# Decode attention: how the last of eight head groups is normalised, turned into rows and written

## The chip, the cores and the metric

The kernel runs on one core of a Trainium2 chip. The metric is the device time in microseconds (us) of one execution. The experiments ran on several chips: b2, a2, rows16 and early28 on chip 7, hyb, pet, w4q and join3 on chip 1, stride8 and a3 on chip 5, probe on chip 6; for the first result none is recorded. Each ratio is taken against the kernel before on the same chip.

A profile covers a "span", from the first to the last instruction. It is 1.8 us shorter than the device time (634.0 against 635.79 in the profiled run of the kernel before). In profiles PE is the matmul engine (TensorE) and PEld its weight load, DVE is VectorE, ACT ScalarE, POOL GpSimd and SP SyncE; a "q" marks an engine's sequencer, which waits and issues DMAs. L195 is line 195 of that run's kernel, so the same step has different line numbers in different runs.

## The reference

One query position, 32 query heads, 8 key/value heads, 65536 keys of 128 elements, bf16:

```python
B, Hq, Hkv, Sq, Sk, D = 1, 32, 8, 1, 65536, 128
...
k = jnp.repeat(k, rep, axis=1)          # rep = 4
v = jnp.repeat(v, rep, axis=1)
scores = jnp.einsum("bhqd,bhkd->bhqk", q, k) * D ** -0.5
p = _softmax(scores, axis=-1)
return jnp.einsum("bhqk,bhkd->bhqd", p, v)
```

The work is reading 268 MB of K and V once. Four query heads share one K/V head; below, "head" with its index `h` of 0 to 7 is such a group of R = 4 query heads. Each is done in C = 2 blocks of 32768 keys, so there are N = 16 blocks. The two blocks of a head are joined with the usual rescaling of a running softmax.

## The kernel before

Each block's products p·V are summed in PSUM (the memory that matmuls write to) as *columns*: 128 partitions (the elements d of the output) by 4 (the query heads). V is the stationary operand (128x128 weights), the probabilities are the 4 moving columns:

```python
def values(tiles):
    for t in tiles:
        ins = pe.matmul(
            acc[:, 0:R], lhsT=vbuf[:, t * D:(t + 1) * D], rhs=pts[:, t * R:(t + 1) * R],
            start=t == 0, stop=t == T - 1,
        )
        if t % TH == TH - 1:
            ins.then_inc(pv_s, 1)
```

The last V block's second half is loaded in five pieces of 64, 32, 16, 8 and 8 tiles (`VLAST`), so that few products are left when the last byte lands. In the kernel before, the last 16 tiles change form: they are summed as *rows* (4 partitions by 128), with the probabilities stationary and V moving, so that the result can be written without a transpose. The columns collected so far are added by a matmul with an f32 identity, the sum of the probabilities is made by a matmul with ones:

```python
pe.matmul(acc[:, 0:R], lhsT=zero, rhs=zero[:, 0:R], start=False, stop=True)
pe.matmul(fsum[0:R, 0:1], lhsT=rhead, rhs=ones, start=True, stop=True).then_inc(fo_s, 1)
for n, a, b in list(pieces(VLAST, TH))[-NROW:]:
    pe.wait_ge(vlast_in[n], 16)
    for t in range(a, b):
        ins = pe.matmul(
            row[0:R, 0:D], lhsT=pts[:, t * R:(t + 1) * R], rhs=vbuf[:, t * D:(t + 1) * D],
            start=t == T - TG, stop=t == T - 1,
        )
    if n == len(VLAST) - NROW:
        pe.wait_ge(co_s, N)
        pe.matmul(row[0:R, 0:D], lhsT=o2, rhs=ident, start=False, stop=False)
ins.then_inc(pv_s, 1)
```

The other 7 heads (28 query heads) are transposed by VectorE in 32x32 blocks and written some 20 us before the end, by four writes from ScalarE's queue. The last head is scaled by ScalarE and written as 4 rows of 256 B:

```python
ac.wait_ge(ox_s, 1)
for a in range(A):                                   # A = 4
    ac.dma_start(
        of[0:Hq - R, a * S4:(a + 1) * S4], oX[a * S4:a * S4 + Hq - R, :],
    ).then_inc(o_out, 16)
ac.wait_ge(rc_s, H)
ac.wait_ge(pv_s, 2 * N)
ac.activation(olast, row[0:R, 0:D], AF.Copy, scale=rrow[0:R, :]).then_inc(ol_s, 1)
ac.wait_ge(ol_s, 1)
ac.dma_start(of[Hq - R:Hq, :], olast).then_inc(o_out, 16)
ac.wait_ge(o_out, 16 * (A + 1))
```

## Time and profile before

| | |
|---|---|
| time | 636.11 us, median of 3 runs (636.04 to 636.58) |
| span of the profiled run | 634.0 us |
| bytes | 268 MB, 424 GB/s |
| busy: PE, DVE, ACT | 43%, 54%, 44% |

The kernel is bound by its loads. Two lines of the page say so: the busy share of the 16 DMA engines in 40 equal slices of the span (a digit is tenths, 9 is 90% or more), and the shares of the chain of work that ended last.

```profile
DMA  9999999999999999999999999999999999999995
...
DMA 48%; DVE 27%; PE 15%; another core or an unknown queue 9%; issue 1%; SPq 1%; POOL 0%; ACT 0%; ACTq 0%
```

Only the last slice is not full. What the change touches all lies there, or is hidden. So the part to read is the chain of waits at the end (start in us, length in us, what it was; "issue" is time in which the engine waited for nothing that the profile shows):

```profile
614.09 14.69 DMA vbuf<-in_v_dram
628.78 0.05 issue
628.83 0.59 PE acc L195 x16
629.42 0.09 issue
629.50 0.16 PE acc L243
629.67 0.12 PE fsum L244 x2
629.79 0.87 PE row L248 x8
630.66 0.43 PE row L254 x2
631.09 0.87 PE row L248 x8
...
632.04 0.36 ACT ktb L408
```

and the same stretch in the timeline (start, length, engine, line, operation, output and inputs, their shapes, count):

```profile
628.83 0.59 PE L195 MATMUL acc<-pts,vbuf 128*128 128x4 bf16 x16 [0.22 <-DMA vbuf<-in_v_dram]
...
629.65 1.01 PE L248 MATMUL row<-vbuf,pts 128*4 128x128 bf16 x8
...
630.46 0.63 PE L254 MATMUL row<-ktb,small 128*4 128x128 f32 x2
...
630.89 1.06 PE L248 MATMUL row<-vbuf,pts 128*4 128x128 bf16 x8
632.04 0.36 ACT L408 ACTIVATE ktb<-row,small 4x128 bf16<-4x128 f32 x1 [15.65 <-PE row L248]
632.43 0.26 ACTq L410 DMA_DIRECT2D out_dram<-ktb  x1
```

A row product is slow: 8 of them take 1.01 to 1.06 us, where 16 column products take 0.59 (one row product starts every 107 ns, one column product every 27 ns). The trace also records when each DMA engine reports its share of a transfer as complete (a "landing"). The last V piece landed at 630.06 us; 15 of its 16 engines had landed by 627.77. From the last landing to the end of the span it is 3.93 us. I call this the *tail*; it is the part of the kernel that the change is meant to shorten:

| part of the tail, before | us |
|---|---|
| last V landing (630.061) to last matmul (631.945) | 1.88 |
| last matmul to issue of the last write (632.43) | 0.49 |
| issue to the write's last landing (633.58) | 1.15 |
| landing to the end of the span (633.995) | 0.41 |

### The profile page before, as it was taken

What the parts mean: (1) busy time and instruction counts of PE and PEld (TensorE: products, weight loads), DVE (VectorE), ACT (ScalarE), POOL (GpSimd) and SP (SyncE); (2) the same over time, 40 slices, a digit from 0 to 9 for tenths busy, and PEclk for the clock granted to TensorE, in tenths of its full rate; (3) what the DMA queues carried; (4) which work ended last, traced back from release to release, by engine and by line L of the source; (5) the groups of instructions that cost most, each with busy time, mean ns of one, the idle gap of its engine ahead of it and who ended that gap; (6) DMA issues with size and microseconds to landing.
All of it is one profiled execution on the core that took longest, in us unless ns stands there. A gap on an engine that the chain in (4) does not pass through costs nothing.

```text
span 634.0 us, 18764 instructions
## 1 busy us (share of the span) xinstructions
PE 271.7 (43%) x8197; PEld 245.2 (39%) x8197; DVE 341.0 (54%) x411; ACT 276.2 (44%) x1179; POOL 10.3 (2%) x33
## 2 busy tenths in 40 slices
PE   1314536144361534626255261553614437146535
PEld 1214436144361433525245261452614436146425
DVE  4649166390853809447193571926619176295710
ACT  1456425164351734617255261542616426165720
POOL 0000000000000000000000000000000000000000
DMA  9999999999999999999999999999999999999995
GB/s 365 429 450 418 443 430 435 438 426 438 422 447 426 438 426 435 438 422 447 418 455 418 442 431 426 442 422 443 422 455 410 451 426 434 430 410 437 430 359 219
DMA packets 6867, 268.68 MB, mean 424 GB/s; under 512 B 1088, under 2 KB 1088, under 8 KB 1728
## 3 DMA queue, kind: packets, MB, share of 16 engines
q1 hardware_dynamic: 6480, 268.44, 98.4%
q8 instruction: 5, 0.08, 0.1%
q14 instruction: 14, 0.11, 0.0%
q10 hardware_dynamic: 368, 0.04, 0.0%
HBM read 268.47 MB, written 0.01 MB: 423 GB/s over the span
## 4 chain that ended last, share of the span: by engine, by line
DMA 48%; DVE 27%; PE 15%; another core or an unknown queue 9%; issue 1%; SPq 1%; POOL 0%; ACT 0%; ACTq 0%
DMA kbuf<-in_k_dram 30%; DVE ktb L284 25%; DMA vbuf<-in_v_dram 17%; PE acc L195 13%; PE qkb L184 2%; DVE small L291 1%; SPq L119 1%; PE row L248 0%; POOL small L165 0%; PE row L254 0%; DVE small L335 0%; ACT ktb L408 0%; DVE small L317 0%; DVE small L313 0%
## 5 line engine op out<-in xcount | busy, mean ns | idle before, releaser
L284 DVE STREAM_TRANSPOSE ktb<-kbuf 128x1024 int32<-128x1024 int32 x256 | 295.8, 1213 | 161.2 <-DMA kbuf<-in_k_dram 158.2
L375 ACT ACTIVATE scs<-qkb 32x64 f32<-32x64 f32 x1024 | 220.5, 215 | 281.3 <-PE qkb L184 270.1
L184 PE MATMUL qkb<-qblk,ktb 128*128 x4096 | 157.3, 176 | 343.0 <-DVE ktb L284 330.3
L184 PEld LDWEIGHTS qkb<-qblk,ktb 128*128 128x128 bf16 x4096 | 132.9, 105 | 367.2 <-issue 199.0
L195 PE MATMUL acc<-pts,vbuf 128*128 128x4 bf16 x4080 | 112.0, 166 | 17.2 <-DMA vbuf<-in_v_dram 16.7
L195 PEld LDWEIGHTS acc<-pts,vbuf 128*128 128x128 bf16 x4080 | 110.4, 104 | 18.9 <-DMA vbuf<-in_v_dram 15.1
L291 DVE TENSOR_REDUCE small<-scs 128x4 f32<-128x256 f32 x64 | 38.0, 593 | 61.4 <-ACT scs L375 61.4
L392 ACT ACTIVATE pts<-scs,small 128x256 bf16<-128x256 f32 x64 | 48.9, 852 | 34.8 <-PE acc L195 34.8
L160 POOL PARTITION_ALL_REDUCE small<-small x16 | 6.0, 372 | 574.8 <-DVE small L302 574.8
L392 ACT ACTIVATION_READ_ACCUMULATOR pts<-scs,small 128x1 f32 x64 | 13.6, 212 | 0.0
L325 DVE COPY small<-acc 128x4 f32<-128x4 f32 x8 | 1.3, 162 | 22.3 <-PE acc L195 22.3
L381 ACT ACTIVATE small<-small 128x4 f32<-128x4 f32 x16 | 3.3, 205 | 21.8 <-POOL small L160 21.8
L313 DVE TENSOR_TENSOR small<-small 128x4 f32<-128x4 f32 x8 | 1.3, 163 | 18.1 <-PE acc L195 18.1
L331 DVE TENSOR_TENSOR small<-acc,small 128x4 f32<-128x4 f32 x8 | 1.2, 155 | 13.0 <-PE fsum L244 13.0
L408 ACT ACTIVATE ktb<-row,small 4x128 bf16<-4x128 f32 x1 | 0.4, 358 | 15.7 <-PE row L248 15.7
L307 DVE TENSOR_TENSOR small<-small 128x4 f32<-128x4 f32 x8 | 1.3, 164 | 4.0 <-POOL small L160 4.0
L165 POOL PARTITION_ALL_REDUCE small<-small x7 | 3.0, 432 | 18.5 <-DVE small L317 18.5
L302 DVE TENSOR_REDUCE small<-small 128x4 f32<-128x16 f32 (+1 forms) x16 | 2.9, 184 | 0.6
L335 DVE RECIPROCAL small<-small 128x4 f32<-128x4 f32 x7 | 1.2, 178 | 3.4 <-POOL small L165 3.4
L315 DVE TENSOR_TENSOR small<-small 128x4 f32<-128x4 f32 x8 | 1.3, 156 | 2.7 <-ACT pts L392 2.7
L365 ACT ACT_TABLE_LOAD x1 | 1.3, 1283 | 2.7 <-issue 2.7
L248 PE MATMUL row<-vbuf,pts 128*4 128x128 bf16 x16 | 2.1, 308 | 0.0
(27 smaller groups left out, 11.4 us busy)
## 6 DMA issues: line engine op xcount, KB each, us to landing
vbuf<-in_v_dram SPq DMA_DIRECT2D x3, 4096.0 KB, 25.5
kbuf<-in_k_dram SPq DMA_DIRECT2D x5, 2048.0 KB, 40.6
kbuf<-in_k_dram SPq DMA_DIRECT2D x1, 4096.0 KB, 22.4
vbuf<-in_v_dram SPq DMA_DIRECT2D x1, 2048.0 KB, 11.8
kbuf<-in_k_dram SPq DMA_DIRECT2D x2, 512.0 KB, 4.8
kbuf<-in_k_dram SPq DMA_DIRECT2D x1, 1024.0 KB, 7.3
vbuf<-in_v_dram SPq DMA_DIRECT2D x1, 1024.0 KB, 13.9
vbuf<-in_v_dram SPq DMA_DIRECT2D x1, 512.0 KB, 14.7
```

The costliest lines, as they stand in the source:

```text
L119: sp.dma_start(buf[:, a * D:b * D], src(t, i)[:, a * D:b * D]).then_inc(s, 16)
L160: g.partition_all_reduce(mtot if b else mfirst, hmax[:, b * R:(b + 1) * R], P, bass.bass_isa.ReduceOp.max,).then_inc(hma_s, 1)
L165: g.partition_all_reduce(lsum, rhead, P, bass.bass_isa.ReduceOp.add).then_inc(ls_s, 1)
L184: ins = pe.matmul(qkb[g // GU][:, at:at + A * R], lhsT=kt[:, be // NE, be % NE, n * P:(n + 1) * P], rhs=qblk[:, bass.ds(qcols[be], A * R)] ...
L195: ins = pe.matmul(acc[:, 0:R], lhsT=vbuf[:, t * D:(t + 1) * D], rhs=pts[:, t * R:(t + 1) * R], start=t == 0, stop=t == T - 1,)
L248: ins = pe.matmul(row[0:R, 0:D], lhsT=pts[:, t * R:(t + 1) * R], rhs=vbuf[:, t * D:(t + 1) * D], start=t == T - TG, stop=t == T - 1,)
L284: dv.transpose(to.rearrange("p (b t j) -> p b t j", b=NB, t=TG), fr.rearrange("p (t b i) -> p b t i", b=NB, t=TG),).then_inc(tr_s, 1)
L291: dv.tensor_reduce(hp[j % C][:, u * R:(u + 1) * R], scs[:, u * W:(u + 1) * W].rearrange("p (n g) -> p g n", g=R), AX.X, ALU.max,).then_inc ...
L302: dv.tensor_reduce(hmax[:, b * R:(b + 1) * R], hp[b].rearrange("p (u g) -> p g u", g=R), AX.X, ALU.max,).then_inc(hm_s, 1)
L375: ins = ac.activation(to[a * S4:(a + 1) * S4, x, :, :], fr[x * S4:(x + 1) * S4, a, :, :], AF.Copy)
L381: ac.activation(negb[b], mtot if b else mfirst, AF.Copy, scale=-scale).then_inc(nb_s, 1)
L392: ac.activation(pv[:, g_, :], sv[:, g_, :], AF.Exp, bias=negb[b][:, g_:g_ + 1], scale=scale, accum_out=rsum[h % 2][b][:, g_:g_ + 1],).then ...
```

## The change

All heads end as columns. The last two pieces use the same column products as the others. The first block's rescaled part joins PSUM by a matmul with the identity as weights, before these two pieces. The sum of the probabilities uses the partition all-reduce of the other heads. Then one multiply, one transpose of all 32 heads and one write from SyncE's (SP's) queue. The four early writes, the row form, the sum by matmul and ScalarE's scaling are gone. The intent is a shorter tail: cheap products at the end, and one write where there were five. The core of the diff:

```diff
@@ sync
+        sp.wait_ge(ox_s, 1)
+        sp.dma_start(of.rearrange("h (a i) -> a h i", a=A), oX).then_inc(o_out, 16)
+        sp.wait_ge(o_out, 16)
@@ gpsimd (... the all-reduce in a helper `total`, called once more at the end)
+        total(H - 1)
@@ tensor
-        pe.wait_ge(tail_s, 3)
-        pe.wait_ge(rh_s, H)
-        pe.matmul(acc[:, 0:R], lhsT=zero, rhs=zero[:, 0:R], start=False, stop=True)
-        pe.matmul(fsum[0:R, 0:1], lhsT=rhead, rhs=ones, start=True, stop=True).then_inc(fo_s, 1)
-        for n, a, b in list(pieces(VLAST, TH))[-NROW:]:
+        pe.wait_ge(tail_s, 2)
+        pe.wait_ge(ow_s, H)
+        pe.matmul(acc[:, 0:R], lhsT=ident, rhs=o2, start=False, stop=False)
+        for n, a, b in list(pieces(VLAST, TH))[-NEND:]:
             pe.wait_ge(vlast_in[n], 16)
-            for t in range(a, b):
-                ins = pe.matmul(row[0:R, 0:D], ...)
-            if n == len(VLAST) - NROW:
-                ...
-        ins.then_inc(pv_s, 1)
+            values(range(a, b))
@@ vector
-        dv.wait_ge(fin_s, H - 1)
+        weigh(H - 1)
+        dv.wait_ge(ls_s, H)
+        dv.reciprocal(recip, lsum).then_inc(rc_s, 1)
+        dv.wait_ge(rc_s, H)
+        dv.wait_ge(pv_s, 2 * N)
+        dv.tensor_tensor(oT[:, Hq - R:Hq], acc[:, 0:R], recip, ALU.mult).then_inc(fin_s, 1)
+        dv.wait_ge(fin_s, H)
         dv.transpose(oX, oT).then_inc(ox_s, 1)
-        collect(N - 1)
-        dv.reciprocal(rrow[0:R, :], fsum[0:R, 0:1]).then_inc(rc_s, 1)
@@ scalar
-        (the four early writes, the scaling and the write of the last head, as shown above)
```

More of the change, by code (lines that the diff above doesn't have):

```diff
@@ L22 @@
 VLAST = (64, 32, 16, 8, 8)
-NROW = 2
+NEND = 2
 HALVED = 2
@@ L41, in bass_standalone__gqa_softmax__decode_kernel @@
     scale = float(D) ** -0.5
-    assert sum(VLAST) == TH and sum(VLAST[-NROW:]) == TG
+    assert sum(VLAST) == TH and sum(VLAST[-NEND:]) == TG
     kf, vf = k[0], v[0]
@@ L74, in bass_standalone__gqa_softmax__decode_kernel @@
     rsum = [[cols(R) for _ in range(C)] for _ in range(2)]
-    warm, ones, rrow = cols(10), cols(1), cols(1)
+    warm = cols(10)
     assert used[0] <= 160
@@ L80, in bass_standalone__gqa_softmax__decode_kernel @@
     ident = ktb[0][:, 0:2 * P].bitcast(DT.float32)
-    zero = ktb[1][:, 0:P]
-    olast = ktb[1][0:R, P:P + D]
     qkb = [S(nc.psum_tensor(f"qkb{i}", [P, 512], DT.float32)) for i in range(U)]
     acc = S(nc.psum_tensor("acc", [P, 512], DT.float32))
-    row = S(nc.psum_tensor("row", [P, 512], DT.float32))
-    fsum = S(nc.psum_tensor("fsum", [P, 512], DT.float32))
     def sem(name):
@@ L101, in bass_standalone__gqa_softmax__decode_kernel @@
         sem("ls_s"), sem("co_s"), sem("ow_s"), sem("rw_s"), sem("rh_s"), sem("rc_s"), sem("fin_s"))
-    fo_s, ol_s, ox_s, tail_s = sem("fo_s"), sem("ol_s"), sem("ox_s"), sem("tail_s")
+    ox_s, tail_s = sem("ox_s"), sem("tail_s")
     init_s, pool_s, qt_s, qb_s, warm_s = sem("init_s"), sem("pool_s"), sem("qt_s"), sem("qb_s"), sem("warm_s")
@@ L149, in _, with total @@
             load_v(j - 1)
+        sp.wait_ge(ox_s, 1)
+        sp.dma_start(of.rearrange("h (a i) -> a h i", a=A), oX).then_inc(o_out, 16)
+        sp.wait_ge(o_out, 16)
     @block.gpsimd
     def _(g):
+        def total(h):
+            g.wait_ge(rh_s, h + 1)
+            g.partition_all_reduce(lsum, rhead, P, bass.bass_isa.ReduceOp.add).then_inc(ls_s, 1)
         g.wait_ge(init_s, 2)
         g.partition_all_reduce(warm[:, 4:8], warm[:, 0:4], P, bass.bass_isa.ReduceOp.max).then_inc(pool_s, 1)
-        g.memset(ones, 1.0).then_inc(pool_s, 1)
         g.memset(oTX[:, :], 0.0).then_inc(pool_s, 1)
@@ L163, in _ @@
             if b == 0 and n >= C:
-                g.wait_ge(rh_s, n // C)
-                g.partition_all_reduce(lsum, rhead, P, bass.bass_isa.ReduceOp.add).then_inc(ls_s, 1)
+                total(n // C - 1)
         g.wait_ge(qk_s, N * G)
-        g.memset(zero, 0.0).then_inc(tail_s, 1)
         g.memset(ident, 0.0).then_inc(tail_s, 1)
-        g.wait_ge(tail_s, 2)
+        g.wait_ge(tail_s, 1)
         g.affine_select(
@@ L232, in _ @@
                 pe.wait_ge(vb_in, late_ * 16)
-                for n, a, b in list(pieces(VLAST, TH))[:-NROW]:
+                for n, a, b in list(pieces(VLAST, TH))[:-NEND]:
                     pe.wait_ge(vlast_in[n], last_ * 16)
@@ L238, in _ @@
             pe.reg_add(turn, turn, 1)
-        pe.wait_ge(tail_s, 3)
-        pe.wait_ge(rh_s, H)
-        pe.matmul(acc[:, 0:R], lhsT=zero, rhs=zero[:, 0:R], start=False, stop=True)
-        pe.matmul(fsum[0:R, 0:1], lhsT=rhead, rhs=ones, start=True, stop=True).then_inc(fo_s, 1)
-        for n, a, b in list(pieces(VLAST, TH))[-NROW:]:
-            pe.wait_ge(vlast_in[n], 16)
-            for t in range(a, b):
-                ins = pe.matmul(
-                    row[0:R, 0:D], lhsT=pts[:, t * R:(t + 1) * R], rhs=vbuf[:, t * D:(t + 1) * D],
-                    start=t == T - TG, stop=t == T - 1,
-                )
-            if n == len(VLAST) - NROW:
-                pe.wait_ge(co_s, N)
-                pe.matmul(row[0:R, 0:D], lhsT=o2, rhs=ident, start=False, stop=False)
-        ins.then_inc(pv_s, 1)
+        pe.wait_ge(tail_s, 2)
+        pe.wait_ge(ow_s, H)
+        pe.matmul(acc[:, 0:R], lhsT=ident, rhs=o2, start=False, stop=False)
+        for n, a, b in list(pieces(VLAST, TH))[-NEND:]:
+            pe.wait_ge(vlast_in[n], 16)
+            values(range(a, b))
     @block.vector
@@ L321, in collect @@
             h, b = divmod(i, C)
-            if i < N - 1:
-                dv.wait_ge(pv_s, (i + 1) * 2)
+            dv.wait_ge(pv_s, (i + 1) * 2)
             if b == 0:
@@ L327, in collect @@
             weigh(h)
-            if i == N - 1:
-                dv.wait_ge(fo_s, 1)
             dv.wait_ge(ow_s, h + 1)
             dv.tensor_tensor(o2, acc[:, 0:R], o2, ALU.add).then_inc(co_s, 1)
-            if i == N - 1:
-                return
             dv.wait_ge(ls_s, h + 1)
@@ L400, in _ @@
             exponent(j)
-        ac.wait_ge(ox_s, 1)
-        for a in range(A):
-            ac.dma_start(
-                of[0:Hq - R, a * S4:(a + 1) * S4], oX[a * S4:a * S4 + Hq - R, :],
-            ).then_inc(o_out, 16)
-        ac.wait_ge(rc_s, H)
-        ac.wait_ge(pv_s, 2 * N)
-        ac.activation(olast, row[0:R, 0:D], AF.Copy, scale=rrow[0:R, :]).then_inc(ol_s, 1)
-        ac.wait_ge(ol_s, 1)
-        ac.dma_start(of[Hq - R:Hq, :], olast).then_inc(o_out, 16)
-        ac.wait_ge(o_out, 16 * (A + 1))
     es.close()
```

## The prediction

> **What bounds it now.** The loads. The page gives DMA 9 tenths in 39 of 40 slices, 424 GB/s; the chain of waits is 48% DMA. PE is 43% busy, DVE 54%, ACT 44%. The change rewrites only the tail after the last loads, so I price that from the timeline and the DMA landings (span 634.0 us).
>
> The last V pieces land on 16 engines, one late: the 16-tile piece at 628.78, the first 8-tile piece at 629.43, the last at 630.06 (15 engines had that last piece by 627.77).
>
> **Tail before** (timeline): acc x16 ends 629.42; clearing matmul (L243), sum matmul (L244), then 8 row matmuls 629.65 to 630.66, the f32 join (L254) 630.46 to 631.09, 8 row matmuls 630.89 to 631.96.  ACT scales at 632.04 (0.36), the write is issued 632.43 (0.26), first packet 633.17, landed 633.58, end 634.00. From the last load to the last matmul: 1.90 us, since row matmuls of 128 columns come every 94 to 123 ns, while the acc form runs 64 in 1.84 us (28 ns each).
>
> **Tail after, estimated from those numbers.**
> - acc x16 ends 629.42. The identity join, two f32 passes with 128x128 weights: 0.3 to 0.5 us, estimated from L254's 128 ns weight loads and L244's 0.19 for two passes. It ends near 629.9, before the last piece lands: hidden.
> - First 8 tiles end about 630.2. Last piece 630.06, its 8 tiles: 8 x 28 ns plus 0.14 drain (as x16 took 0.59) end near 630.48.
> - DVE multiply by the reciprocal 0.16 (L331's size) plus semaphore, transpose 0.20 (L355): oX ready near 630.93.
> - SP issues one write of 128 rows of 64 B: 0.43 (SP's other issues of 128 rows; 4 rows took 0.26). Start to first packet 0.74 for 4 rows, 1.0 for the 128-row first load; I take 0.95. Each of 16 engines does 8 packets of 11 ns (the early 64 B writes), landing 0.35 later: about 632.45. The closing barrier 0.42: end 632.85.
>
> Row matmuls: 1.9 us shrinks to 0.4; ACT's 0.36 becomes DVE's 0.4 in two steps; the write costs about 0.3 more. Net about -1.1 us, all on the critical path. All-reduce of the last sums (0.43) and the reciprocal (0.18) move to about 617, off the path (last rhead is at 616.8).
>
> Removed too: four early writes (112 rows of 64 B, beside the last V loads). The late engine's 16 packets of 8192 B from 620.11 to 625.04 took 16 x 309 ns, so they seem to cost it nothing.
>
> The Trainium skill, "DMA: Bandwidth & Descriptors", "Why a DMA increments its semaphore by 16 and not by 1", says the engine count comes from the row count: 128 rows use 16, 4 rows use 4; the trace agrees, the last write has 4 landings. Its "Specifications" says writes under 512 B are read-modify-write; 64 B rows may land later than 256 B ones. No isolated one is in the trace: the largest doubt.
>
> **Prediction: 635.0 us** against 636.11, range 634.3 to 636.0. Faster by over 2%: 0.005; within 2%: 0.99; slower: 0.005.
>
> **Right or wrong shows in:** L195 matmuls ending about 0.4 us after the last landing; last packet-to-landing near 0.35; no ACT work after 617; span near 632.9.
>
> **What would make it wrong:** instruction fetches (8192 B, 309 ns) fall differently on the late engine, moving the last landing by 0.3 us steps; the join costs over 0.6 us; the 128-row write lands 0.5 us later.

## The result, and the profile after

The changed kernel took 636.0 us (median of 6 runs, 635.65 to 636.23) against 636.12 us (6 runs, 635.97 to 636.58). The ratio is 0.9997, 95% interval 0.9984 to 1.0009: no difference that these runs can show. (A ratio is the mean time of one kernel's runs over that of the other's of the same rounds, so not quite the ratio of the medians quoted.) Instead of the forecast gain of 1.1 us, 0.1 us was seen. The profiled span was even longer, 634.3 us against 634.0.

The end of the changed kernel's chain of waits:

```profile
614.28 15.34 DMA vbuf<-in_v_dram
629.62 0.05 issue
629.67 0.59 PE acc L196 x16
630.26 0.10 issue
630.36 0.56 PE acc L244 x2
630.92 0.44 PE acc L196 x16
...
631.45 0.17 DVE oTX L346
631.62 0.02 issue
631.65 0.21 DVE oTX L348
```

and its timeline:

```profile
630.36 0.56 PE L244 MATMUL acc<-small,ktb 128*128 128x4 f32 x2
...
630.77 0.57 PE L196 MATMUL acc<-pts,vbuf 128*128 128x4 bf16 x16
631.45 0.16 DVE L346 TENSOR_TENSOR oTX<-acc,small 128x4 bf16<-128x4 f32 x1 [13.72 <-PE acc L196]
631.65 0.21 DVE L348 STREAM_TRANSPOSE oTX<-oTX 128x32 bf16<-128x32 bf16 x1
631.88 0.68 SPq L147 DMA_DIRECT2D out_dram<-oTX  x1
```

Two things are to be seen. First, the DMA line at the top of the chain ends at 629.62 and not at 628.78: that is the landing of the 16-tile piece, and the last piece follows in the same way, at 630.90 and not at 630.06. The loads ended 0.84 us later, though nothing in the loads was changed. Second, the last matmul ends at 631.34 (before: 631.95) in spite of that, but the write is issued for 0.68 us, not for 0.26, and lands late:

| part of the tail | before | predicted | after |
|---|---|---|---|
| last V landing to last matmul | 1.88 | 0.42 | 0.44 |
| last matmul to issue of the write | 0.49 | 0.45 | 0.54 |
| issue to the write's last landing | 1.15 | 1.52 | 2.02 |
| landing to end | 0.41 | 0.40 | 0.39 |
| sum (the tail, us) | 3.93 | 2.79 | 3.40 |

(The sums are taken from the unrounded times. The predicted column subtracts the times that the prediction gives: 630.06, 630.48, 630.93 (transposed rows ready, taken as the issue), 632.45, 632.85.) So 1.45 us were won at the products, and 0.87 us were given back at the write. The span adds the 0.84 us of the later landing: 634.0 - 0.54 + 0.84 = 634.3.

### The profile page after: what moved, and what is told of

It reads as the page before. It is cut to its first block, busy times and chain, and to the rows that moved or that the text cites. A ratio compares the mean times of both kernels' runs of the same rounds, so it can differ in the third digit from the quotient of the medians.

```text
span 634.3 us, 18751 instructions
## 1 busy us (share of the span) xinstructions
PE 269.9 (43%) x8194; PEld 243.9 (38%) x8194; DVE 341.1 (54%) x411; ACT 275.7 (43%) x1178; POOL 10.5 (2%) x32
## 4 chain that ended last, share of the span: by engine, by line
DMA 48%; DVE 27%; PE 14%; another core or an unknown queue 9%; SPq 1%; issue 1%; POOL 0%; DVEq 0%
DMA kbuf<-in_k_dram 30%; DVE ktb L276 25%; DMA vbuf<-in_v_dram 17%; PE acc L196 13%; PE qkb L185 1%; DVE small L283 1%; SPq L115 1%; POOL small L154 0%; PE acc L244 0%; DVE small L322 0%; DVE small L309 0%; DVE small L305 0%; DVE oTX L348 0%; DVE oTX L346 0%
## 5 line engine op out<-in xcount | busy, mean ns | idle before, releaser
L372 ACT ACTIVATE small<-small 128x4 f32<-128x4 f32 x16 | 3.3, 205 | 21.7 <-POOL small L162 21.7
L305 DVE TENSOR_TENSOR small<-small 128x4 f32<-128x4 f32 x8 | 1.3, 163 | 18.3 <-PE acc L196 18.2
L299 DVE TENSOR_TENSOR small<-small 128x4 f32<-128x4 f32 x8 | 1.3, 163 | 4.0 <-POOL small L162 4.0
L307 DVE TENSOR_TENSOR small<-small 128x4 f32<-128x4 f32 x8 | 1.3, 157 | 2.7 <-ACT pts L383 2.7
L375 ACT ACTIVATE small<-small 128x4 f32<-128x4 f32 x8 | 1.6, 205 | 0.0
L309 DVE TENSOR_TENSOR small<-small 128x4 f32<-128x4 f32 x8 | 1.3, 163 | 0.3
```

Of the source, the lines that this page charges most:

```text
L372: ac.activation(negb[b], mtot if b else mfirst, AF.Copy, scale=-scale).then_inc(nb_s, 1)
L375: ac.activation(wgt, dif, AF.Exp, scale=scale).then_inc(wg_s, 1)
```

## The experiments

The theories, as the expectations name them:

- **Theory A**: the time of the last V landing wanders from run to run, whatever the tail does. **Rival, theory B**: the change delays it.
- **Theory W**: the write is slow by its shape. Its four landings, and 132 packet records in the trace (128 rows and 4 completion marks), show that it ran on 4 engines, 32 rows each. **Rivals**: many small rows are slow however they are spread; a single late write is slow whatever its shape; the column form itself costs.

The Trainium skill, "DMA: Bandwidth & Descriptors", section "Why a DMA increments its semaphore by 16 and not by 1", states that the number of engines is the largest k up to 16 that divides the slowest dimension, other than 1, of *both* access patterns. The source here is 128 partitions, but the destination `"h (a i) -> a h i"` has `a` = 4 outermost. So k = 4, and the trace agrees.

### b2 and a2: both kernels again

No edit. Theory A against theory B.

> The kernel before, unchanged, for a second profile. Theory A (the time at which the last V piece lands wanders by some tenths of a us from run to run, whatever the tail does): the last landing, 630.06 in the first profile, differs by 0.2 to 0.8 us, and from there to the end it is again 3.9 us. Theory B (the change itself delays the last landing): 630.1 within 0.2 us again.

> The changed kernel, unchanged, for a second profile and a tighter ratio. Theory A: the last landing, 630.90 in the first profile, moves by 0.2 to 0.8 us, mostly earlier; from it to the end it is again 3.4 us; ratio 0.9992 (0.5 us saved). Theory B: 630.9 within 0.2 us again, ratio 0.9998.

| | last V landing | tail | time, median of 5 | ratio to before |
|---|---|---|---|---|
| before, first profile | 630.06 | 3.93 | | |
| b2 | 630.46 | 3.94 | 636.10 | 0.9996 (0.9982 to 1.0009) |
| after, first profile | 630.90 | 3.40 | | |
| a2 | 630.41 | 3.39 | 635.61 | 0.9988 (0.9974 to 1.0002) |

Theory A holds: one and the same kernel differs by 0.40 (before) and 0.49 us (after) between its two profiles. In the second pair the order of the landings is even turned round (630.46 and 630.41), while the two tails repeat within 0.01 us. (Two profiles of each can't exclude a small delay by the change; all profiles together are set side by side below.) The tail is thus the measure that tells kernels apart, and the change shortens it by 0.54 us. In these rounds the plain times don't overlap either: 635.34 to 635.87 for a2, 635.96 to 636.66 for all runs of the kernel before. The interval of the ratio is wider and just reaches 1. The end of a2's timeline, to be set beside the one above: every step is the same, half a us earlier.

```profile
630.96 0.16 DVE L346 TENSOR_TENSOR oTX<-acc,small 128x4 bf16<-128x4 f32 x1 [13.19 <-PE acc L196]
631.15 0.21 DVE L348 STREAM_TRANSPOSE oTX<-oTX 128x32 bf16<-128x32 bf16 x1
631.39 0.68 SPq L147 DMA_DIRECT2D out_dram<-oTX  x1
```

### rows16: the same write on 16 engines

```diff
-        sp.dma_start(of.rearrange("h (a i) -> a h i", a=A), oX)
+        sp.dma_start(of.rearrange("h (a i) -> (h a) i", a=A), oX)
```

The same 128 rows of 64 B go to the same 8 KB, in another order, so the result is wrong. The destination's slowest dimension is now 128.

> The changed kernel with the rows of its one write in another order in DRAM (wrong result on purpose): the destination's slowest dimension is then 128 and not 4. Theory W (the write is slow because it runs on 4 engines with 32 packets each, and because its issue takes 0.68 us): 16 landings, issue 0.43 us, from issue to last landing 1.45 us instead of 2.03, the run 0.5 us shorter than the changed kernel. Rival (128 rows of 64 B are slow whatever the spread, by the small writes themselves): 16 landings but 1.9 to 2.1 us, same time.

The result was wrong (relative error 0.44). There were 16 landings, 1.41 us from issue to the last one, and the tail was 2.79 us, which is the predicted tail of the change. 634.97 us, ratio 0.9980 (0.9966 to 0.9994). The issue is short again:

```profile
631.22 0.35 SPq L147 DMA_DIRECT2D out_dram<-oTX  x1
```

Small rows as such are not what makes the write slow: 128 rows of 64 B cost 1.41 us when the pattern is plain. The order of the destination costs 0.61 us. It shows in the plain times too: the five runs of rows16 took 634.81 to 635.21 us, those of a2 in the same rounds 635.34 to 635.87. The packet records say where:

| us | before (4 rows of 256 B) | a2 (128 rows, 4 engines) | rows16 (128 rows, 16 engines) |
|---|---|---|---|
| issue to first packet | 0.74 | 1.27 | 0.84 |
| first packet to end of the last | 0.08 | 0.29 | 0.21 |
| end of the last to last landing | 0.33 | 0.46 | 0.36 |
| sum | 1.15 | 2.02 | 1.41 |

0.43 of the 0.61 us come before the first byte, and only 0.18 while the packets run and land. This did not yet tell whether the number of rows for each engine or the form of the pattern makes the issue long (see stride8).

### early28: the early writes back, four small ones at the end

```diff
+        dv.transpose(oX, oT).then_inc(ox_s, 1)     # after 7 heads; ACT writes 28 rows x 4 early, as before
...
-        sp.dma_start(of.rearrange("h (a i) -> a h i", a=A), oX)
+        # last head, transposed into its own tile oL; a = 0, 2 from SP, a = 1, 3 from ACT
+        dma_start(of[Hq - R:, a * S4:(a + 1) * S4], oL[(a + 1) * S4 - R:(a + 1) * S4, :])
```

> The changed kernel with the four early writes of 28 heads back, and at the end only four writes of 4 rows of 64 B, two from SP and two from ACT. Theory W: last write from first issue to last landing 1.4 us, so 0.6 us less than the changed kernel, 635.4. Theory B in the form that the removed early writes delayed the last landing: landing back at 630.1 and 0.8 us more gained, 634.6. Theory A: last landing anywhere from 630.0 to 631.0.

Correct. The last V landing was at 630.31, inside the range of the runs without early writes, so the form of theory B that blames their removal has nothing for it. From the first issue to the last landing it was 1.67 us, not the 1.4 expected: the second issue on each queue begins 0.29 to 0.39 us after the first. Tail 3.04 us; 635.38 us, ratio 0.9986 (0.9972 to 1.0000).

### hyb: the products of the change, the write of before

The change's column products and join are kept, but the writes are those of the kernel before. The 4 columns are turned into 4 rows by one bf16 identity matmul:

```diff
+        pe.wait_ge(fin_s, H)
+        pe.matmul(row[0:R, 0:D], lhsT=oT[:, Hq - R:Hq], rhs=identb, start=True, stop=True).then_inc(fo_s, 1)
...
-        dv.transpose(oX, oT).then_inc(ox_s, 1)
+        dv.tensor_copy(olast, row[0:R, 0:D]).then_inc(ox_s, 1)
...
+        sp.dma_start(of[Hq - R:, :], olast).then_inc(o_out, 16)     # 28 heads early, as before
```

> The column products and the join of the changed kernel, but the writes of the kernel before (28 heads early by four writes, the last head as 4 rows of 256 B): the 128x4 result is turned into rows by one bf16 identity matmul. One part of the change alone. Theory W: issue to landing 1.15 us again as in the kernel before, last matmul of V 0.44 us after the last landing as in the changed kernel; tail from the last V landing to the end 2.85 us against 3.94 before and 3.39 changed; time 0.5 us under the changed kernel. Rival (the column form is what costs, not the write): tail 3.4 or more.

Correct. Issue to landing was 1.18 us, as in the kernel before, and the last V product ended 0.43 us after the last landing, as in the changed kernel. So the column form does not cost; the write does. The tail was 3.02 us and not 2.85, because the turn into rows is dear: a matmul of 0.27 and a cast of 0.28 us (DVE's transpose takes 0.21), and with the waits between them 1.02 us from the last V product to the issue, against 0.54 in the changed kernel. The time was 0.2 us under a2's (on another chip), not the 0.5 expected.

```profile
631.14 0.16 DVE L356 TENSOR_TENSOR oTX<-acc,small 128x4 bf16<-128x4 f32 x1 [13.40 <-PE acc L201]
...
631.45 0.27 PE L255 MATMUL row<-ktb,oTX 128*4 128x128 bf16 x1 [0.41 <-DVE oTX L356]
631.75 0.28 DVE L358 CAST ktb<-row 4x128 bf16<-4x128 f32 x1 [0.45 <-PE row L255]
632.06 0.35 SPq L150 DMA_DIRECT2D out_dram<-ktb  x1
```

635.41 us, ratio 0.9987 (0.9973 to 1.0000).

### pet: one write of all heads as 32 plain rows

As hyb, but the identity matmul turns all 32 heads, there are no early writes, and one write takes 32 rows of 256 B:

```diff
-        sp.dma_start(of.rearrange("h (a i) -> a h i", a=A), oX)
+        sp.dma_start(of, oall)                      # oall: 32 partitions x 128
```

> The changed kernel with its 32x32 transpose replaced by one identity matmul of all heads, so that the one write has 32 rows of 256 B, slowest dimension 32. Theory W: 16 landings, issue 0.35 us, issue to last landing 1.2 us; tail 2.9 us. Rival (one write of all heads at the end is slow whatever its shape): 1.7 us or more, tail 3.4.

Correct. 16 landings, issue 0.36 us, issue to last landing 1.38 us (1.2 expected). One late write of all heads is thus not slow as such. Beside rows16's 1.41 us it also shows that 8 rows of 64 B for each engine cost about what 2 rows of 256 B do. The tail of 3.24 us missed the 2.9 expected, mostly by the turn into rows, again 1.02 us from the last V product to the issue. 635.64 us, ratio 0.9992 (0.9979 to 1.0006).

### w4q: four plain writes of 32 rows, on two queues

```diff
-        sp.dma_start(of.rearrange("h (a i) -> a h i", a=A), oX)
+        # a = 0, 2 from SP, a = 1, 3 from ACT
+        dma_start(of[:, a * S4:(a + 1) * S4], oX[a * S4:(a + 1) * S4, :])
```

> The changed kernel with its one write cut into four of 32 rows of 64 B, two from SP and two from ACT. Each has slowest dimension 32 and so 16 engines. Theory W: 1.7 us from first issue to last landing (1.41 as in the reordered write, plus 0.35 for the second issue on each queue), tail 3.05 us. Rival (64 B writes are what is slow, not the spread): 2.0 us, tail 3.4.

Correct, but a miss for the expectation: 1.99 us from the first issue to the last landing and a tail of 3.36 us, the numbers that were written down for the rival. The rival's reason is not borne out, though, as rows16 writes the same 64 B rows in 1.41 us. The trace shows each queue's two issues taking 0.36 to 0.45 us and the second starting 0.41 us after the first; from the later second issue to the last landing it is still 1.57 us. Why this is 0.16 us more than rows16's 1.41 was not looked into. Cutting one write into four costs about as much as the bad order does. 635.49 us, ratio 0.9989 (0.9976 to 1.0003).

### join3: the identity join one piece earlier

```diff
-NEND = 2
+NEND = 3          # and the tiles kept out of the loop: sum(VLAST[-NEND:]) in place of TG
```

> The changed kernel with the identity join one piece earlier, before the 16-tile piece. If the join (0.56 us) is hidden behind the wait for the last piece, as predicted, the last matmul ends again 0.44 us after the last landing and the tail is again 3.4 us. Rival (the join delays the last products, as the chain of waits has it in its list): 0.3 us less of both.

Correct (one look; a single run has no rated state, 635.44 us). The join moved out of the way: it ends at 629.41, and PE then waits 0.25 us for the last piece.

```profile
628.85 0.56 PE L245 MATMUL acc<-small,ktb 128*128 128x4 f32 x2
...
630.30 0.38 PE L197 MATMUL acc<-pts,vbuf 128*128 128x4 bf16 x8 [0.25 <-DMA vbuf<-in_v_dram]
```

The last matmul still ended 0.42 us after the last landing, and the tail was 3.37 us. So the join of 0.56 us is hidden, although the chain of waits of the changed kernel lists it: PE was working on it while the last piece was on its way, and no more than 0.02 us of it shows in the tail, which is within the 0.03 us by which tails repeat.

### stride8: few rows, but the same two-step pattern

28 heads are written early. The last head's 4 columns are put 8 apart before the transpose, so that its 16 rows lie 8 partitions apart and one write takes them:

```diff
-        dv.tensor_tensor(oT[:, Hq - R:Hq], acc[:, 0:R], recip, ALU.mult).then_inc(fin_s, 1)
+        dv.tensor_tensor(spread, acc[:, 0:R], recip, ALU.mult).then_inc(fin_s, 1)   # columns 0, 8, 16, 24
...
+        sp.dma_start(of[Hq - R:, :].rearrange("h (a i) -> a h i", a=A), oL[0:P:S4 // R, :])
```

> 28 heads written early as in the kernel before; the last head's 4 columns are put 8 apart before the 32x32 transpose, so that its 16 rows of 64 B lie 8 partitions apart and one write takes them, again on 4 engines as the changed kernel's write but with 4 packets each in place of 32. Theory W with the row count as the cost (32 rows an engine make the issue and the packets long): issue 0.3 us, issue to last landing 1.2 to 1.3 us, tail 2.65 us, time 1.2 us under before. Rival (a pattern that steps both over a and h is slow in itself, at 0.68 us to issue): issue to landing 1.7 us or more, tail 3.1.

Correct. Here theory W, in the form that blames the number of rows, fell for the larger part. With 4 rows on each engine instead of 32 the issue is as long as in the changed kernel:

```profile
631.68 0.67 SPq L149 DMA_DIRECT2D out_dram<-oL  x1
```

From issue to first packet it was 1.27 us, exactly as with 128 rows; the packets took 0.09 (0.29) and the landing 0.33 (0.46). Sum 1.69 us; tail 3.12 us; 635.45 us, ratio 0.9987 (0.9974 to 1.0001). So of the 0.87 us that the write gives back against the kernel before, 0.53 go with the form of the pattern (a destination that steps over `a` and then over `h`), before the first byte. 0.33 go with the 32 rows for each engine. The use of only 4 engines does not explain the first part: hyb's write also ran on 4 engines, and from the same SP queue it was issued in 0.35 us and had its first packet after 0.77. Nor does the step of 8 partitions in stride8's source, which the changed kernel does not have, with the same 1.27 us. What in the two-step pattern takes the time was not separated further. The plain write of 128 rows on 16 engines has 0.10, 0.13 and 0.04 us more than before in the three parts.

### a3: the changed kernel beside stride8

> The changed kernel once more, beside the run above on the same chip: tail from the last V landing 3.4 us, last landing between 630.1 and 631.0, time 0.5 us under before.

Tail 3.42 us, last landing 630.46, 635.71 us, ratio 0.9991 (0.9978 to 1.0005). All as expected.

### probe: which engine is late

In every profile one engine lands the last piece 1.6 to 2.9 us after the next. The probe puts 14 tiny loads of 1 to 14 rows behind the last V piece on the same queue:

```diff
+        for m in range(1, 15):
+            sp.dma_start(kbuf[0][0:m, m * 32:m * 32 + 32], src(vf, 0)[0:m, 0:32]).then_inc(pr_s[m - 1], 16)
```

> The changed kernel with 14 tiny loads of 1 to 14 rows of 64 B behind the last V piece on SP's queue. In all profiles the last V piece lands on 15 engines by 628.6 and on one near 630.5. If a load of k rows runs on the k lowest engines and each engine works its queue in order, the loads with k up to some e land by 629 and all with more rows land after the last V piece, near 631: then the late engine is number e. If instead all land alike, engines do not keep that order, or the late engine is not among the first 14. The tail stays 3.4 us, counted from the last V landing.

The write waits for the tiny loads here, so the span and tail say nothing about the kernel; that part of the expectation was careless (the tail was 4.84 us). The landings (last V piece: 15 engines by 627.91, the last at 630.42):

```
rows   first    ...  next to last   last landing
1      627.37
2      627.55                       630.60
3      627.57        627.73         630.77
4      627.74        628.09         630.94
8      627.25        628.85         631.64
14     626.86        629.93         632.68
```

The load of one row is not late, that of two rows has one late landing, and so has each larger one. The late engine is the second one, number 1, if the loads use the lowest-numbered engines, as the skill's section named above states; the nested pattern fits that, but the trace does not number the engines. The same page, section "Latency and other measured facts", has engines 7 and 15 as the usual slow ones, with a guess at the cause that concerns DMAs issued from GpSimd; these loads are issued from SP. In this one run, on chip 6, it is neither of them. Which engine was late in the other profiles is not shown.

### The tails together

| run | V landing to last V product | issue to landing | tail, us |
|---|---|---|---|
| before, b2 | 1.88, 1.90 | 1.15, 1.15 | 3.93, 3.94 |
| after, a2, a3 | 0.44, 0.43, 0.47 | 2.02, 2.02, 2.02 | 3.40, 3.39, 3.42 |
| join3 | 0.42 | 2.02 | 3.37 |
| w4q | 0.44 | 1.99 | 3.36 |
| pet | 0.45 | 1.38 | 3.24 |
| stride8 | 0.46 | 1.69 | 3.12 |
| early28 | 0.44 | 1.67 | 3.04 |
| hyb | 0.43 | 1.18 | 3.02 |
| rows16 (wrong result) | 0.46 | 1.41 | 2.79 |

No correct version reached 2.79 us. A single DMA in the right order with `h` outermost would have to step over partitions in two dimensions at its source; no such run was made. The best correct ones, early28 and hyb, have tails about 0.9 us shorter than before and 0.37 us shorter than the change. By their times they are 0.13% to 0.14% under before, with intervals that just reach 1; against the changed kernel the times alone do not separate them.

## Why the prediction was right or wrong

The measured 636.0 us lies at the very edge of the stated range (634.3 to 636.0), and "within 2%" was right. Neither says much: the point was 1.0 us off, and 2% of the time is 12.7 us, three times the whole tail. The size of the gain was not right: 1.1 us was forecast, and 0.1 us was measured in the first six pairs of runs. The changed kernel's later runs were 0.72 and 0.45 us under before by their medians (a2, a3). The tail, which repeats within 0.03 us, gives 0.54 us.

- **The bound and where to look**: right. The kernel is bound by its loads, and only what follows the last landing counts.
- **Products**: right. "L195 matmuls ending about 0.4 us after the last landing" was measured at 0.43 and 0.44 (a2 and the first profile).
- **The join**: right that it is hidden (join3), slightly too cheap at 0.3 to 0.5 us (0.56). It was to end 0.16 us before the last landing; in the first profile after it ended 0.02 us behind it (630.92 against 630.90), so nothing was to spare.
- **The sums off the path, no ACT work after 617**: right. The all-reduce ran at 617.08 for 0.43 us, the reciprocal at 617.55 for 0.18 us, and ACT's last record ends at 616.58.
- **Multiply and transpose**: right within 0.1 us (0.54 against 0.45 us from the last matmul to the issue).
- **The early writes cost nothing**: nothing speaks against it. With them the last landing was at 630.06, 630.46, 630.31, 630.61 and 630.63 (before, b2, early28, hyb, stride8), without them at 630.90, 630.41, 630.22, 630.47, 630.29, 630.25 and 630.46 (after, a2, rows16, pet, w4q, join3, a3). The means are 630.41 and 630.43.
- **The write**: this is the step that failed. The prediction put it as "SP issues one write of 128 rows of 64 B: 0.43", "I take 0.95" to the first packet, and "Each of 16 engines does 8 packets". It read the engine count from the source's 128 rows alone. The rule looks at both patterns, and the destination begins with `a` = 4. It also had no term for the destination's two-step pattern, which is the larger part: 0.43 of the 0.61 us that separate this write from rows16's come before the first byte, and the number of engines does not account for them (hyb, stride8). In place of these numbers the runs show an issue of 0.68, 1.27 us to the first packet, 4 engines with 32 packets each, 0.46 us from the last packet to the last landing instead of "near 0.35", and 2.02 us in all instead of about 1.5. With the write that the prediction had in mind (rows16) the tail came out at 2.79 us, as predicted; that the sum agrees so well is partly luck, as its parts are off by 0.04, 0.09, -0.11 and -0.02 us and cancel. The prediction's worry, small rows landing late, was not what happened; only its guess of 0.5 us more was right in size.
- **The last landing**: it was named as a risk ("moving the last landing by 0.3 us steps") and it came, 0.84 us later in the first pair of profiles. As far as the profiles tell, it belongs to the run and not to the change: over all of them it lies between 630.06 and 630.90. The reason named, instruction fetches on the late engine, was not shown. Near 618 us every profile has one fetch of 8192 B. It took 707 ns where the landing was early (630.06), 309 ns where it was latest (630.90), and 821 ns in between (630.41); in join3 it took 309 ns again and the landing was early (630.25). So its length does not go with the landing. Its start does: it is 617.78 us in the first profile before, 618.79 in that after, and within these bounds in all others (correlation with the landing of that half block 0.88 over the 13 profiles), which may be a cause or another sign of the same delay. The difference arises in the load of the first half of the last V block. From the previous block's last landing to this half's it was 10.52 us in the first profile of before, 11.22 in that of after, 10.72 and 10.68 in b2 and a2. Why it varies, and why one engine is late at all, stays open. Also open is why the first six timed runs of the changed kernel were 0.3 to 0.4 us slower in the median than its later ones; a later last landing, as in one profile, would account for it, but the other five have no profile. The spans fit that: less a tail of 3.40 us, the six spans of 633.9 to 634.4 us put the last landing at 630.5 to 631.0, and a2's five, 633.5 to 634.1, at 630.1 to 630.7. These are estimates, which take the tail as constant.

## What to carry to other kernels

When the end of a kernel is a chain of short steps behind the last load, measure it from the last landing and not from the start: this tail repeated within 0.03 us, where the whole time wandered by more than the gain. Price a final write by *both* of its access patterns: here the destination's outermost dimension of 4 left 4 engines in use although the source had 128 rows, and the two-step destination order cost 0.4 to 0.5 us before the first byte. A step that the chain of waits lists is not always worth its length: the 0.56 us join, moved out of the way, won no more than 0.02 us.

## What the Trainium skill lacked or had wrong

- "DMA: Bandwidth & Descriptors", "Specifications", gives a first-byte latency of about 0.6 us for DMAs from the SP and ACT queues. From the start of the issue it was 0.74 us (4 rows), 0.84 us (128 rows, plain order) and 1.27 us (a destination that steps over two dimensions, with 16 rows as with 128). Counted from the end of the issue it was 0.48, 0.49 and 0.60 us, so the page's figure is not contradicted; it does not say from where it counts. It has nothing on a two-step pattern, whose issue alone took 0.67 to 0.68 us where the single plain writes at the end took 0.26 to 0.36.
- The same page, "Latency and other measured facts": engines 7 and 15 as the usual slow ones. In every profile here one engine was late at the last load, by 1.6 to 2.9 us; in the one run that tested which (probe), it was number 1, if engines are taken in the page's order.
- The same page, "Specifications", has transfers under 512 B as read-modify-write. No run here tests that, as all rows written are under 512 B. The entry gives no ground for a difference between 64 B and 256 B rows, and on 16 engines hardly any was seen: 1.41 against 1.38 us from issue to last landing for the same 8 KB.
- The same page's rule for the number of engines held in every write that was looked at: 4 landings where the smaller slowest dimension was 4, 16 for 32 and 128, and 14 for each of the four early writes of 28 rows (56 in all). Nothing to mend there; it was I who read it for the source alone.
